# Feeding one stage of a fused attention and gMLP block: eight operand pieces reloaded in place, or twelve in two rings

## The chip, the core and the metric

The kernel runs on one NeuronCore of one Trainium2 chip. The metric is device time in microseconds, of one launch.

## What is computed

One transformer block with two parallel branches on 2048 tokens of width 512, in float32:

```python
xn = layernorm(x)                                   # x: 2048 x 512
q, k, v = split(xn @ wqkv)                          # 32 heads of 16
A = softmax(q @ k.T * 16**-0.5) @ v, heads joined, @ wo
z = gelu(xn @ w_in)                                 # 2048 x 1792
z1, z2 = z[:, :896], layernorm(z[:, 896:])
B = (z1 * (w_sp @ z2 + b_sp)) @ w_out               # w_sp: 2048 x 2048
out = x + A + B
```

## The kernel before

Dense products are made in three float32r passes (high times high, low times high, high times low), each operand held as a high and a low part. The contraction of 128 rows is cut into an upper and a lower half of 64 rows, which run side by side in PE as two matmuls into two PSUM banks, `dps0` and `dps1`. One such pair of matmuls is a *slot* (`dense_slot`, L1456).

Two streams of work share PE. Attention goes through 16 pairs of heads, each with four groups of 512 queries and 16 steps: maxima (M, L1405), scores (S, L1391), exponentials on ACT, and value products (V, L1499). The dense stream is a queue of generators: the values' projection, q and k (`qk_rest`), z2 (`z2_all`, 16 token tiles), z1 (`z1_all`), the product with w_sp (`spatial`), w_out (`mlp_out`) and wo (`attn_out`). The strings `ORDER` say by hand in which order S, M, V and dense slots (D) follow each other; one string is a row, and each row ends in a V.

The whole program is laid out ahead of time by a planner in Python. It keeps an estimated clock for each engine (`T`), and writes an instruction when its planned time has come; loads are asked for by small generators, which wait for room in a pool of buffers (`piece`, `room`), for a *road* that spaces large loads (`clear`, `bulk`), or for a planned time (`later`). The chip then keeps to the written order on each engine, and only semaphores decide when an instruction starts. All loads and nearly all stores go through SP's one queue (`move`, L169), in the order written. In the built program each transfer of that queue waits for the landing of the one eight places before it, so eight are under way at most.

The stage around the change is z1: z1 transposed, 896 rows in seven blocks of 128 (f), by four groups g of 512 tokens. `W1 = ((0, 1), (2, 3), (4, 5), (6, 6))` pairs the blocks: unit u works on two blocks, one in the upper half of PE's rows and one in the lower. Units 0 to 2 take both blocks from the same g; unit 3, the odd block 6, takes group g-1 in the upper half and g in the lower, once for each odd g. So the order of units is 0 1 2 (g = 0), 3 0 1 2 (g = 1), 0 1 2 (g = 2), 3 0 1 2 (g = 3): 14 units of eight steps j. A step needs the piece `xp` j of the normalised, transposed x: 64 upper rows for one block and 64 lower rows for the other, each a load of 256 KB from DRAM (`xscr`), and a half of the unit's weights `w1p` (two loads of 256 KB from `w1scr`).

There are eight buffers `xp0` to `xp7`. `fetch_first` (L628) fills them once, beginning with the last of z2's tiles. Afterwards `x_next` (L615) reloads an upper or a lower half in place, right after the step that used it last: the lower halves after unit 2 of an even g, the upper halves after unit 3, both after unit 2 of an odd g. `xat[j]` is the planned time at which piece j is in (`LOADX` = 6.0 us after its issue). The eight `w1p` pieces are asked for by `fetch_w1` (L619) from three tiles before the end of z2 on, all of them ahead of x. At the same time other loads pass through SP's queue: at each change of the pair of heads eight parts of the next pair's *stacks* (`qst`, `kst`, `load_stacks` L926), once per group the row maxima of the scores, which DVE makes (`ms`), and which go out (`mscr<-ms`) and come back in two loads into the rows of q (`qst<-mscr`, `max_fin` L955), the stores of z2 and z1 (`z2scr`, `z1scr`), and eight kept pieces of w_sp (`fetch_parts`, `wf<-wsscr`, 512 KB each).

Of the kernel before, what the change touches and what calls it, by code (L numbers as in the profile page):

```python
# [22 lines left out]
NT = S // P  # L23
# [60 lines left out]
LOADX = 6.0  # L84
# [9 lines left out]
def fused_block(ctx, tc, x, wqkv, wo, w_in, w_spT, b_sp, w_out, out):  # L94
# [76 lines left out]
    def clock():  # L171
        return T["P"]
# [195 lines left out]
    def fetch_parts(out, k, scr, spare):  # L368
        yield "C", lambda: clear() and room["big"] + room["old"] > 1 + spare[0]
        bulk(2.0)  # L370
# [236 lines left out]
    xp, xat = {}, {}  # L607

    def x_half(g, j, rows):
        c, h = divmod(j, 2)  # L610
        for r in rows:
            move(xp[j][64 * r:64 * r + 64], xscr[g][c][64 * h:64 * h + 64])
        xat[j] = max(clock(), ends[0]) + LOADX

    def x_next(g, j, rows):  # L615
        xat[j] = FAR
        later(0.2, x_half, g, j, rows)

    def fetch_w1(u, i, spare):  # L619
        yield "C", lambda: clear() and room["big"] + room["old"] > 1 + spare[0]  # L620
        bulk(2.0)
        t = piece(f"w1p{u}_{i}", place(w1, (u, i)))
        for r, f in enumerate(W1[u]):
            move(t[64 * r:64 * r + 64].rearrange("p a (c h f) -> p a c h f", c=2, h=2), w1scr[:, f, :, 2 * i:2 * i + 2, :, :])
        yield "T", LOAD
        w1[u, i] = t

    def fetch_first():  # L628
        for j in range(2 * ND):
            yield "C", lambda: room["big"] + room["old"] > 2  # L630
            xp[j] = piece(f"xp{j}", place(xp, j))
            x_half(0, j, (0, 1))
        late1[0] = 1

    def z2_all():
        yield from need(lambda: len(w2) == 2 * ND)
        for t in range(NT):
# [6 lines left out]
            if t == NT - 3:  # L644
                for u in range(4):
                    for i in range(2):
                        spawn(fetch_w1(u, i, late1), 1)
            if t == NT - 1:
                spawn(fetch_first(), 1)
# [52 lines left out]
    def z1_all():  # L702
        for g in range(NG):
# [3 lines left out]
            for n, (u, lo, hi) in enumerate(pairs):  # L707
# [9 lines left out]
                yield from need(lambda: (u, 0) in w1 and (u, 1) in w1)  # L717
                for j in range(2 * ND):
                    yield from need(lambda: xat.get(j, FAR) <= clock(), 0.1)
                    c = slice(j % 4 * P, (j % 4 + 1) * P)  # L720
                    ops = lambda _: (w1[u, j // 4][:, 0, c], w1[u, j // 4][:, 1, c], xp[j][:, 0, :], xp[j][:, 1, :])
                    yield from dense(1, ops, ops, (0, 1), j == 0, j == 2 * ND - 1)
                    if u == 3:
                        x_next(g, j, (0,))
                    elif u == 2 and g == NG - 1:
                        later(0.7, leave, xp, j)
                    elif u == 2:
                        x_next(g + 1, j, (0, 1) if g % 2 else (1,))
# [899 lines left out]
```

## Time and profile before

| | |
|---|---|
| three runs | 1828.26, 1833.22, 1839.35 us (median 1833.22) |
| profiled execution | 1831.37 us, of which 1829.3 from the first to the last instruction |
| granted clock of PE over the span | 0.996 |
| busy: PE, DVE, ACT, POOL | 1790.8, 1443.7, 1212.6, 685.3 us |
| matmuls of z1 (`dps<-xp,w1p`) | 672, from 500.7 to 694.4 us |
| loads of x halves for z1 (`xp<-xscr`) | 64 of 256 KB, issued from 488.4 to 654.0 us |

A busy time is the union of an engine's instructions, so PE's 98% says that something runs on it, not that it runs at its peak. What one stage costs is read from that stage: from the distance between the same points of the schedule there and elsewhere, and from what ended each wait. In the rows of waits and of the timeline, the bracket at the end gives the idle time before the instruction and what ended it. "SPq" is SP's queue issuing a transfer; that row's duration is the issuing, not the transfer.

### The profile page before, as it was taken

What the parts mean: (1) busy time and instruction counts of PE and PEld (TensorE: products, weight loads), DVE (VectorE), ACT (ScalarE), POOL (GpSimd) and SP (SyncE); (2) the same over time, 40 slices, a digit from 0 to 9 for tenths busy, and PEclk for the clock granted to TensorE, in tenths of its full rate; (3) what the DMA queues carried; (4) which work ended last, traced back from release to release, by engine and by line L of the source; (5) the groups of instructions that cost most, each with busy time, mean ns of one, the idle gap of its engine ahead of it and who ended that gap; (6) DMA issues with size and microseconds to landing.
All of it is one profiled execution on the core that took longest, in us unless ns stands there. A gap on an engine that the chain in (4) does not pass through costs nothing.

```text
span 1829.3 us, 38128 instructions
## 1 busy us (share of the span) xinstructions
PE 1790.8 (98%) x14708; PEld 1083.9 (59%) x14708; DVE 1443.7 (79%) x1716; ACT 1212.6 (66%) x1329; POOL 685.3 (37%) x803
## 2 busy tenths in 40 slices
PE   9999999999999999999999999999999999999997
PEld 6665665665665556666565665656566565664542
DVE  8868788888887777888788777878778787887882
ACT  4357777888876767666666666666666666666655
POOL 5442142777787767222722270007020600011201
PEclk9999999999999999999999999999999999999999
DMA  7879854434987676775878497548856766583322
GB/s 265 285 229 310 260 182 111 131 109 121 241 200 223 159 190 176 195 174 164 225 188 197 140 223 169 140 121 223 183 143 175 206 158 146 135 199 96 105 87 81
DMA packets 257757, 323.18 MB, mean 177 GB/s; under 512 B 70096, under 2 KB 147472, under 8 KB 257568
## 3 DMA queue, kind: packets, MB, share of 16 engines
q1 hardware_dynamic: 250088, 293.49, 61.0%
q0 software_dynamic: 7488, 27.27, 4.6%
q8 instruction: 115, 1.88, 0.4%
q14 instruction: 66, 0.54, 0.1%
HBM read 206.36 MB, written 114.30 MB: 175 GB/s over the span
## 4 chain that ended last, share of the span: by engine, by line
PE 89%; DMA 4%; DVE 4%; ACT 1%; POOL 1%; issue 1%; SPq 0%; POOLq 0%; DVEq 0%; ACTq 0%
PE dps L1456 35%; PE sl L1499 24%; PE sl L1391 14%; PE sl L1405 12%; DVE mm L950 3%; DMA xp<-xscr 2%; DMA kst<-kscr 1%; ACT pf L111 1%; PE dps L1470 1%; PE sl L277 1%; PE sl L278 0%; PE sl L279 0%; DMA w1p<-w1scr 0%; PE sl L1456 0%; DVE bst L1175 0%
## 5 line engine op out<-in xcount | busy, mean ns | idle before, releaser
L950 DVE TENSOR_REDUCE mm<-sl 128x2 f32<-128x1024 f32 x1008 | 1207.2, 1222 | 182.3 <-PE sl L1405 172.4
L111 ACT ACTIVATE pf<-sl 128x1024 f32<-128x1024 f32 x1024 | 1042.9, 1026 | 347.2 <-PE sl L1391 309.8
L1391 PE MATMUL sl<-qst,kst 50*128 50x512 f32 x2048 | 433.8, 416 | 8.0 <-DVE mm L950 2.9
L1499 PE MATMUL sl<-pf,vhalf 128*32 128x512 f32 x3840 | 439.8, 597 | 0.9 <-DVE on L1085 0.7
L1405 PE MATMUL sl<-kst,qst 48*128 48x512 f32 x2016 | 416.0, 404 | 5.4 <-ACT pf L111 2.8
L1456 PE MATMUL dps<-wsp,zs 64*128 64x512 f32 x2352 | 382.6, 392 | 0.0
L1391 PEld LDWEIGHTS sl<-qst,kst 50*128 50x128 f32 x2048 | 195.0, 184 | 209.7 <-issue 75.2
L1405 PEld LDWEIGHTS sl<-kst,qst 48*128 48x128 f32 x2016 | 192.3, 185 | 115.7 <-ACT pf L111 53.0
L1499 PEld LDWEIGHTS sl<-pf,vhalf 128*32 128x32 f32 x3840 | 111.7, 110 | 251.4 <-issue 216.2
L1456 PEld LDWEIGHTS dps<-wsp,zs 64*128 64x128 f32 x2352 | 225.8, 187 | 35.6
L111 ACT ACTIVATE e<-sl 128x512 f32<-128x512 f32 x64 | 38.3, 599 | 185.5 <-PE sl L1499 162.0
L1529 DVE TENSOR_TENSOR e<-sl,e 128x512 f32<-128x512 f32 x64 | 44.3, 692 | 133.5 <-PE sl L1499 74.8
L848 POOL TENSOR_TENSOR hhl<-z1i,hhl 128x512 fp32r<-128x512 f32 x26 | 33.2, 1287 | 275.8 <-ACT hhl L111 254.8
L1456 PE MATMUL dps<-xp,w1p 64*128 64x512 f32 x672 | 113.2, 397 | 7.8 <-DMA xp<-xscr 7.8
L1456 PE MATMUL dps<-w,xt 64*128 64x448 f32 x768 | 113.0, 368 | 1.7
L1456 PE MATMUL dps<-wout,hp 64*128 64x512 f32 x672 | 110.1, 392 | 0.0
L1001 POOL TENSOR_TENSOR ob<-ob 128x512 f32<-128x512 f32 (+1 forms) x16 | 20.6, 1287 | 214.1 <-DMA ob<-rscr 195.4
L1456 PEld LDWEIGHTS dps<-w,xt 64*128 64x128 f32 x768 | 75.6, 186 | 15.3 <-issue 8.1
L1456 PEld LDWEIGHTS dps<-xp,w1p 64*128 64x128 f32 x672 | 66.6, 188 | 20.3 <-DMA xp<-xscr 11.0
L1456 PEld LDWEIGHTS dps<-wout,hp 64*128 64x128 f32 x672 | 64.8, 187 | 9.8
L467 POOL TENSOR_TENSOR qkhl<-qr,qkhl 128x512 fp32r<-128x512 f32 x24 | 30.4, 1284 | 85.4 <-ACT qkhl L111 40.5
L997 POOL TENSOR_TENSOR ob<-ob 128x512 f32<-128x512 f32 (+1 forms) x16 | 20.9, 1304 | 100.3 <-DMA ob<-escr 98.5
(252 smaller groups left out, 1618.4 us busy)
## 6 DMA issues: line engine op xcount, KB each, us to landing
zs<-z2scr SPq DMA_DIRECT2D x192, 256.0 KB
xp<-xscr SPq DMA_DIRECT2D x64, 256.0 KB
escr<-e SPq DMA_DIRECT2D x60, 256.0 KB
hscr<-hhl POOLq DMA_DIRECT2D x28, 512.0 KB, 6.8
qst<-qscr SPq DMA_DIRECT2D x60, 192.0 KB
kst<-kscr SPq DMA_DIRECT2D x60, 192.0 KB
qscr<-qkhl SPq DMA_DIRECT2D x16, 512.0 KB
kscr<-qkhl SPq DMA_DIRECT2D x16, 512.0 KB
```

The source lines that it names most:

```text
L111: return nc.scalar.activation(out, in_, func, **kw)
L277: nc.tensor.matmul(acc, lh, rh, start=first, stop=False)
L467: nc.gpsimd.tensor_sub(hl[:, 1, :], raw_, hl[:, 0, :].bitcast(F32))
L848: nc.gpsimd.tensor_sub(hl[:, 1, :], z1, hl[:, 0, :].bitcast(F32))
L950: nc.vector.tensor_reduce(mmax[g][:, :, t, kc], sl[k], AX.X, ALU.max)
L997: nc.gpsimd.tensor_add(both_[rows, 0, :], both_[rows, 0, :], both_[rows, 1, :])
L1001: nc.gpsimd.tensor_mul(both_[rows, 0, :], both_[rows, 0, :], both_[rows, 1, :])
L1391: nc.tensor.matmul(sl[k][:, j, :], kst[p % 2][rows, kt * P:(kt + 1) * P], qst[p % 2][rows, c * 512:(c + 1) * 512], start=True, stop=True)
L1405: nc.tensor.matmul(sl[k][:, j, :], qst[p % 2][rows, tt * P:(tt + 1) * P], kst[p % 2][rows, kc * 512:(kc + 1) * 512], start=True, stop=True)
L1456: nc.tensor.matmul(bank_of(bank)[:, :w], lhs, rhs, start=go, stop=stop)
L1499: nc.tensor.matmul(sl[k][cols:cols + VW, 0, :], vpack(p, kt + r, j), pf[:, j * 512:(j + 1) * 512], start=n % CYC == 0, stop=n % CYC == CYC ...
L1529: nc.vector.tensor_add(e, sl[k][:, 0, :], e)
```

## The change

Twelve buffers `xp0` to `xp11` take the place of eight. The upper halves form one ring over the twelve, the lower halves another: the half for group g and step j is number q = 8 g + j and goes to buffer q modulo 12, and it may be loaded when the half twelve before it has been used for the last time (`xgone`). One generator, `z1_loader`, asks for all 64 halves and the eight `w1p` pieces in the order in which the units need them (`x_due`). It begins four tiles of z2 before the end, not three (weights) or one (x). Each load waits for the planner's road, and takes 1.6 us of it (an x half) or 3.0 us (a weight piece), unless it is due within six steps of the present one. A step waits, in the plan, for the halves and the weights that it uses. `LOADX` goes from 6.0 to 7.0 us, and a kept piece of w_sp takes 3.0 us of the road and not 2.0. The arithmetic and the number of transfers stay.

```diff
-LOADX = 6.0
+LOADX = 7.0
+XRING = 12
+XBULK = 1.6
...
     def fetch_parts(out, k, scr, spare):
         yield "C", lambda: clear() and room["big"] + room["old"] > 1 + spare[0]
-        bulk(2.0)
+        bulk(3.0 if out is wsp else 2.0)
...
-    xp, xat = {}, {}
...
-    def x_next(g, j, rows):
-        xat[j] = FAR
-        later(0.2, x_half, g, j, rows)
-
-    def fetch_w1(u, i, spare):
...
-    def fetch_first():
-        for j in range(2 * ND):
-            yield "C", lambda: room["big"] + room["old"] > 2
-            xp[j] = piece(f"xp{j}", place(xp, j))
-            x_half(0, j, (0, 1))
-        late1[0] = 1
+    xp, xat, slot = {}, {}, []
+    at_x, xgone = [-FAR], [0, 0]
+
+    def x_uses():
+        n = 0
+        for g in range(NG):
+            for u in ((3, 0, 1, 2) if g % 2 else (0, 1, 2)):
+                yield n, u, g - 1 if u == 3 else g, g
+                n += 1
+
+    def x_due():
+        seen, due = set(), []
+        for n, u, *gs in x_uses():
+            for j in range(2 * ND):
+                for r in (0, 1):
+                    if (r, gs[r], j) not in seen:
+                        seen.add((r, gs[r], j))
+                        due.append((8 * n + j, 1, r, 8 * gs[r] + j))
+            for i in range(2):
+                if ("w", u, i) not in seen:
+                    seen.add(("w", u, i))
+                    due.append((8 * n + 4 * i, 0, u, i))
+        return sorted(due)
+
+    def z1_loader():
+        for d, is_x, p, q in x_due():
+            soon = lambda: clear() or d <= at_x[0] + 6
+            if is_x:
+                k, (g, j) = q % XRING, divmod(q, 2 * ND)
+                c, h = divmod(j, 2)
+                yield "C", lambda: soon() and q < xgone[p] + XRING and (k in xp or room["big"] + room["old"] > 1 + late1[0])
+                bulk(XBULK)
+                if k not in xp:
+                    xp[k] = piece(f"xp{k}", place(xp, k))
+                move(xp[k][64 * p:64 * p + 64], xscr[g][c][64 * h:64 * h + 64])
+                xat[p, q] = max(clock(), ends[0]) + LOADX
+            else:
+                yield "C", lambda: soon() and room["big"] + room["old"] > 1 + late1[0]
+                bulk(3.0)
...
+                w1[p, q] = t
...
-            if t == NT - 3:
-                for u in range(4):
-                    for i in range(2):
-                        spawn(fetch_w1(u, i, late1), 1)
+            if t == NT - 4:
+                spawn(z1_loader(), 1)
             if t == NT - 1:
-                spawn(fetch_first(), 1)
+                late1[0] = 1
...
-                yield from need(lambda: (u, 0) in w1 and (u, 1) in w1)
                 for j in range(2 * ND):
-                    yield from need(lambda: xat.get(j, FAR) <= clock(), 0.1)
+                    at_x[0] = 8 * unit + j
+                    pu, pl = 8 * lo + j, 8 * hi + j
+                    yield from need(lambda: all(xat.get(k, FAR) <= clock() for k in ((0, pu), (1, pl), ("w", u, j // 4))), 0.1)
...
+                    xu, xl, wt = xp[pu % XRING], xp[pl % XRING], w1[u, j // 4]
...
-                    if u == 3:
-                        x_next(g, j, (0,))
-                    elif u == 2 and g == NG - 1:
-                        later(0.7, leave, xp, j)
-                    elif u == 2:
-                        x_next(g + 1, j, (0, 1) if g % 2 else (1,))
+                    if u == 3 or u == 2 and lo % 2:
+                        later(0.2, xgone.__setitem__, 0, pu + 1)
+                    if u == 2:
+                        later(0.2, xgone.__setitem__, 1, pl + 1)
```

In the built program DVE's and ACT's instructions stand in the same order as before, and so do PE's matmuls, but for the names of some buffers. What moves is SP's queue. In the rows below `xp`, `w1p`, `xt`, `wf`, `qst` and `kst` are loads, `z2scr`, `z1scr`, `escr` and `mscr` stores, and the first number of a name is that of the buffer or part.

First place: SP's queue at the end of z2, where tile 15's operand (`xt15`) is loaded and the stacks of the next pair follow. Before, from the last row of `xt15` on:

```order
L169 DMA xt15_5346<-xscr3_3_127 128x2x128
L169 DMA z2scr_129<-z2hl9_1_5279 128x3x128
L169 DMA w1p0_0_5355<-w1scr_186 64x2x512 x2
L169 DMA qst0_100<-qscr1_105 48x1024
L169 DMA kst0_102<-kscr1_109 48x1024
L169 DMA w1p0_1_5387<-w1scr_186 64x2x512 x2
L169 DMA qst0_100<-qscr1_105 48x1024
L169 DMA qst1_101<-mscr2_176 2x16x32 x2
L169 DMA w1p1_0_5418<-w1scr_186 64x2x512 x2
L169 DMA kst0_102<-kscr1_109 48x1024
L169 DMA qst0_100<-qscr1_105 48x1024
L169 DMA kst0_102<-kscr1_109 48x1024
```

Now, the rows ahead of `xt15`, and then those behind it:

```order
L171 DMA w1p0_0_5180<-w1scr_186 64x2x512 x2
L171 DMA escr0_0_142<-e3_0_5010 128x512
L171 DMA xp0_5231<-xscr0_0_112 64x1024 x2
L171 DMA xp1_5275<-xscr0_0_112 64x1024 x2
L171 DMA z2scr_129<-z2hl9_0_5205 128x4x128
L171 DMA xp2_5325<-xscr0_1_113 64x1024 x2
L171 DMA z2scr_129<-z2hl9_0_5205 128x4x128
L171 DMA mscr2_176<-ms14_5322 128x32
L171 DMA z2scr_129<-z2hl9_1_5287 128x3x128
L171 DMA xt15_5358<-xscr3_0_124 128x2x128
```

```order
L171 DMA xt15_5358<-xscr3_3_127 128x2x128
L171 DMA z2scr_129<-z2hl9_1_5287 128x3x128
L171 DMA qst0_100<-qscr1_105 48x1024
L171 DMA kst0_102<-kscr1_109 48x1024
L171 DMA qst0_100<-qscr1_105 48x1024
L171 DMA qst1_101<-mscr2_176 2x16x32 x2
L171 DMA kst0_102<-kscr1_109 48x1024
L171 DMA qst0_100<-qscr1_105 48x1024
L171 DMA kst0_102<-kscr1_109 48x1024
L171 DMA z2scr_129<-z2hl10_0_5347 128x4x128
L171 DMA qst0_100<-qscr1_105 48x1024
L171 DMA xp3_5485<-xscr0_1_113 64x1024
```

Half of unit 0's weights and the first three x pieces, both halves, went ahead of `xt15`; no weights of z1 stand among the stacks any more, and the fourth x piece does.

Second place: SP's queue at the change of pair after the first three units of z1, up to the store of the maxima. Before:

```order
L169 DMA xp3_5796<-xscr1_1_117 64x1024
L169 DMA qst1_101<-qscr1_105 48x1024
L169 DMA xp4_5799<-xscr1_2_118 64x1024
L169 DMA xp5_5817<-xscr1_2_118 64x1024
L169 DMA kst1_103<-kscr1_109 48x1024
L169 DMA xp6_5820<-xscr1_3_119 64x1024
L169 DMA qst1_101<-qscr1_105 48x1024
L169 DMA xp7_5829<-xscr1_3_119 64x1024
L169 DMA kst1_103<-kscr1_109 48x1024
L169 DMA qst1_101<-qscr1_105 48x1024
L169 DMA mscr1_175<-ms17_6350 128x32
L169 DMA kst1_103<-kscr1_109 48x1024
```

Now:

```order
L171 DMA qst1_101<-qscr1_105 48x1024
L171 DMA xp2_5325<-xscr1_3_119 64x1024
L171 DMA kst1_103<-kscr1_109 48x1024
L171 DMA xp3_5485<-xscr1_3_119 64x1024
L171 DMA qst1_101<-qscr1_105 48x1024
L171 DMA xp8_6114<-xscr1_0_116 64x1024
L171 DMA xp9_6137<-xscr1_0_116 64x1024
L171 DMA xp10_6159<-xscr1_1_117 64x1024
L171 DMA kst1_103<-kscr1_109 48x1024
L171 DMA qst1_101<-qscr1_105 48x1024
L171 DMA mscr1_175<-ms17_6356 128x32
L171 DMA kst1_103<-kscr1_109 48x1024
```

Before, the lower halves of group 1 (`xscr1`) for `xp0` to `xp7` stand among the stacks, all eight between the end of z2's stores and `mscr`; now four of them do (`xp0` to `xp3`, as numbers 12 to 15), the four others were loaded ahead of the stretch into `xp8` to `xp11`, and three upper halves come before `mscr`, where none came. From the first of these x halves to `mscr` there are 18 transfers before and 16 now; right ahead of them now stands the last weight piece, `w1p3_1`, in two transfers.

Third place: SP's queue at the change of pair in the last group. Before:

```order
L169 DMA qst0_100<-qscr1_105 48x1024
L169 DMA xp4_5799<-xscr3_2_126 64x1024
L169 DMA xp5_5817<-xscr3_2_126 64x1024
L169 DMA kst0_102<-kscr1_109 48x1024
L169 DMA xp6_5820<-xscr3_3_127 64x1024
L169 DMA qst0_100<-qscr1_105 48x1024
L169 DMA wf5_5_7577<-wsscr5_183 128x1024
L169 DMA xp7_5829<-xscr3_3_127 64x1024
L169 DMA kst0_102<-kscr1_109 48x1024
L169 DMA qst0_100<-qscr1_105 48x1024
L169 DMA mscr1_175<-ms21_7604 128x32
```

Now:

```order
L171 DMA xp5_5762<-xscr3_2_126 64x1024
L171 DMA kst0_102<-kscr1_109 48x1024
L171 DMA xp6_5810<-xscr3_3_127 64x1024
L171 DMA qst0_100<-qscr1_105 48x1024
L171 DMA xp7_5847<-xscr3_3_127 64x1024
L171 DMA kst0_102<-kscr1_109 48x1024
L171 DMA wf1_1_7566<-wsscr1_179 128x1024
L171 DMA qst0_100<-qscr1_105 48x1024
L171 DMA wf1_1_7594<-wsscr2_180 128x1024
L171 DMA kst0_102<-kscr1_109 48x1024
L171 DMA qst0_100<-qscr1_105 48x1024
L171 DMA mscr1_175<-ms21_7602 128x32
```

Before, the upper halves of group 3 (`xscr3`) go through the whole stretch, the last one behind a piece of w_sp; now their last one stands ahead of two such pieces, and the first four stand before the stretch. From the first transfer of the stretch (`xp0` before, `z1scr2` now) to `mscr` there are 18 transfers before and 15 now.

More of the change, by code (lines that the diff above doesn't have):

```diff
@@ L606, in fused_block @@
     W1 = ((0, 1), (2, 3), (4, 5), (6, 6))
-    xp, xat = {}, {}
[L609 to L613, printed above, removed]
-    def x_next(g, j, rows):
-        xat[j] = FAR
-        later(0.2, x_half, g, j, rows)
-    def fetch_w1(u, i, spare):
[L620 to L626, printed above, removed]
@@ new lines, in z1_loader @@
+    def z1_loader():
[13 more added lines that the diff above has]
+                bulk(3.0)
+                t = piece(f"w1p{p}_{q}", place(w1, (p, q)))
+                for r, f in enumerate(W1[p]):
+                    move(t[64 * r:64 * r + 64].rearrange("p a (c h f) -> p a c h f", c=2, h=2), w1scr[:, f, :, 2 * q:2 * q + 2, :, :])
+                xat["w", p, q] = max(clock(), ends[0]) + LOAD
+                w1[p, q] = t
@@ L702, in z1_all @@
     def z1_all():
+        unit = 0
         for g in range(NG):
@@ L716, in z1_all @@
                     calm[0] = True
-                yield from need(lambda: (u, 0) in w1 and (u, 1) in w1)
                 for j in range(2 * ND):
-                    yield from need(lambda: xat.get(j, FAR) <= clock(), 0.1)
+                    at_x[0] = 8 * unit + j
+                    pu, pl = 8 * lo + j, 8 * hi + j
+                    yield from need(lambda: all(xat.get(k, FAR) <= clock() for k in ((0, pu), (1, pl), ("w", u, j // 4))), 0.1)
                     c = slice(j % 4 * P, (j % 4 + 1) * P)
-                    ops = lambda _: (w1[u, j // 4][:, 0, c], w1[u, j // 4][:, 1, c], xp[j][:, 0, :], xp[j][:, 1, :])
-                    yield from dense(1, ops, ops, (0, 1), j == 0, j == 2 * ND - 1)
-                    if u == 3:
-                        x_next(g, j, (0,))
-                    elif u == 2 and g == NG - 1:
-                        later(0.7, leave, xp, j)
-                    elif u == 2:
-                        x_next(g + 1, j, (0, 1) if g % 2 else (1,))
+                    xu, xl, wt = xp[pu % XRING], xp[pl % XRING], w1[u, j // 4]
+                    au, al = (wt[:, 0, c], wt[:, 1, c], xu[:, 0, :], xu[:, 1, :]), (wt[:, 0, c], wt[:, 1, c], xl[:, 0, :], xl[:, 1, :])
+                    yield from dense(1, lambda _: au, lambda _: al, (0, 1), j == 0, j == 2 * ND - 1)
+                    if u == 3 or u == 2 and lo % 2:
+                        later(0.2, xgone.__setitem__, 0, pu + 1)
+                    if u == 2:
+                        later(0.2, xgone.__setitem__, 1, pl + 1)
+                    if g == NG - 1 and (u == 2 or u == 3 and pu + XRING >= 2 * ND * NG):
+                        later(0.7, leave, xp, pu % XRING)
                 if g == NG - 1:
@@ L731, in z1_all @@
                         leave(w1, (u, i))
+                unit += 1
                 yield "e", [z1_out(f, h, i) for i, (f, h) in enumerate(zip(W1[u], (lo, hi)))]
```

## The prediction

> **What bounds the kernel now.** I read the page's busy shares and the chain that ended last first, then who PE waited for, then those waits in PE's timeline, and last SP's queue around them.
>
> ```profile
> PE 1790.8 (98%) x14708; PEld 1083.9 (59%) x14708; DVE 1443.7 (79%) x1716; ACT 1212.6 (66%) x1329; POOL 685.3 (37%) x803
> PE 89%; DMA 4%; DVE 4%; ACT 1%; POOL 1%; issue 1%; SPq 0%; POOLq 0%; DVEq 0%; ACTq 0%
> ...
> PE dps L1456 <- DMA xp<-xscr: 7.8, 5, 3.9
> PE sl L1391 <- DMA qst<-mscr: 0.7, 1, 0.7
> ```
>
> PE is the bound: busy for 98% of the span and 89% of the chain. An edit that leaves PE's instructions as they are can therefore only win what PE waits, and the waits on this change's transfers are 7.8 us in five pieces (the last two rows are from the table of who waited for whom: total, times, longest). PE's timeline shows where they stand, in brackets, with a sixth on a row of maxima:
>
> ```profile
> 472.05 0.69 PE L1391 MATMUL sl<-qst,kst 50*128 50x512 f32 x2 [0.67 <-DMA qst<-mscr]
> ...
> 508.24 0.73 PE L1456 MATMUL dps<-xp,w1p 64*128 64x512 f32 x3 [0.52 <-DMA xp<-xscr]
> 510.32 0.50 PE L1456 MATMUL dps<-xp,w1p 64*128 64x512 f32 x2 [0.54 <-DMA xp<-xscr]
> ...
> 551.95 0.50 PE L1456 MATMUL dps<-xp,w1p 64*128 64x512 f32 x2 [1.17 <-DMA xp<-xscr]
> ...
> 567.28 0.50 PE L1456 MATMUL dps<-xp,w1p 64*128 64x512 f32 x2 [1.65 <-DMA xp<-xscr]
> ...
> 664.84 1.22 PE L1456 MATMUL dps<-xp,w1p 64*128 64x512 f32 x4 [3.91 <-DMA xp<-xscr]
> ```
>
> Idle time is not the whole loss, because PE runs slower after a long wait and small waits of the weight loads do not show as PE idle. The whole loss is read from the pitch of the schedule: every row of the hand-written order ends in one block of value matmuls (L1499), so the starts of these blocks are a ruler.
>
> ```profile
> 440.39 3.64 PE L1499 MATMUL sl<-pf,vhalf 128*32 128x512 f32 x32
> ...
> 467.75 2.78 PE L1499 MATMUL sl<-pf,vhalf 128*32 128x512 f32 x24
> ...
> 496.58 3.64 PE L1499 MATMUL sl<-pf,vhalf 128*32 128x512 f32 x32
> 511.68 1.90 PE L1499 MATMUL sl<-pf,vhalf 128*32 128x512 f32 x13
> ...
> 538.45 1.92 PE L1499 MATMUL sl<-pf,vhalf 128*32 128x512 f32 x16
> ...
> 569.14 2.35 PE L1499 MATMUL sl<-pf,vhalf 128*32 128x512 f32 x20 [0.18 <-ACT pf L111]
> ...
> 648.99 1.49 PE L1499 MATMUL sl<-pf,vhalf 128*32 128x512 f32 x12
> ...
> 681.98 2.35 PE L1499 MATMUL sl<-pf,vhalf 128*32 128x512 f32 x20
> ...
> 908.78 1.49 PE L1499 MATMUL sl<-pf,vhalf 128*32 128x512 f32 x12
> ...
> 935.42 1.92 PE L1499 MATMUL sl<-pf,vhalf 128*32 128x512 f32 x16
> ...
> 660.00:680.00 20.00, 16.09 (x118) 8.95 (x118) 10.74 (x10) 10.44 (x13) 9.50 (x10) 0.83 0.86 218
> ```
>
> Two rows take 27.36 us in the z2 stage (440.39 to 467.75) and 26.64 where nothing waits later (908.78 to 935.42). Against that: (a) 467.75 to 496.58 takes 28.83, 1.47 too much, the tail of z2; (b) 496.58 to 511.68, one row, takes 15.10 against 13.68, 1.42 too much, the first unit of z1; (c) 538.45 to 569.14 takes 30.69, 4.05 too much; (d) 648.99 to 681.98 takes 32.99, 6.35 too much. Of (d) 3.91 is the wait; the other 2.44 is PE's clock, which the last row (a window of 20 us: PE, PEld, DVE, ACT, POOL, clock, DMA share, GB/s) gives as 0.83 of full. No wait of 1.65 or less did that. Sum of the losses: 1.47 + 1.42 + 4.05 + 6.35 = 13.29 us.
>
> **Why the transfers are late.** The chain names the issue and the time to landing of the transfers on which PE waited, and SP's queue shows what it held:
>
> ```profile
> 502.46 7.81 DMA xp<-xscr
> ...
> 540.57 11.34 DMA xp<-xscr
> ...
> 560.97 6.27 DMA xp<-xscr
> ...
> 654.03 10.76 DMA xp<-xscr
> ...
> SPq L169 <- DMA xp<-xscr: 21.0, 32, 1.5
> ...
> 440.00:460.00 20.00, 19.48 (x166) 11.60 (x168) 16.91 (x27) 17.08 (x22) 13.68 (x24) 1.00 0.40 113
> 460.00:480.00 20.00, 18.87 (x162) 13.21 (x160) 16.79 (x21) 16.05 (x18) 15.08 (x20) 1.00 1.01 204
> 540.00:560.00 20.00, 18.84 (x156) 11.18 (x150) 13.31 (x15) 13.07 (x16) 18.64 (x25) 1.00 1.01 200
> ...
> 529.93 0.51 SPq L169 DMA_DIRECT2D xp<-xscr  x1
> ...
> 544.86 0.34 SPq L169 DMA_DIRECT2D mscr<-ms  x1
> ...
> 553.82 1.35 SPq L169 DMA_DIRECT2D qst<-mscr  x2
> ...
> 640.60 0.44 SPq L169 DMA_DIRECT2D xp<-xscr  x1
> ...
> 657.56 0.34 SPq L169 DMA_DIRECT2D mscr<-ms  x1
> ...
> 666.28 1.34 SPq L169 DMA_DIRECT2D qst<-mscr  x2
> ```
>
> Issue plus landing gives 510.27, 551.91, 567.24 and 664.79: to within 0.1 us where the waits end. From 529.93 to 540.57 SP issued 16 transfers, and the last landed at 551.91: 1.37 us each, DMA share 1.01 in that window. From 640.60 to 654.03 it issued 16 again, landing at 664.79: 1.51 us each. So z1's pieces stand in a full line, together with the next pair's stacks (qst, kst), and a piece that moves out of that stretch brings all behind it forward by about 1.4 us. SP itself waited 21.0 us in 32 pieces for older xp transfers (window 440 to 700), the sign that its line of eight outstanding transfers was full.
>
> **The change part by part.** PE, DVE and ACT keep their instructions in the same order: DVE's and ACT's are equal row by row, PE's differ only in the names of wsp pieces; POOL moves one store's issue by a place. No engine's work changes: 0 us. The number of transfers stays too (64 x halves, 16 for w1). What moves is SP's line.
>
> - *Twelve pieces instead of eight.* The first four pieces of each next group of 512 columns find room before the old group is used up. Of the eight lower halves that stood between 529.93 and 540.57, four now stand ahead of that stretch: 4 x 1.37 = 5.5 us earlier for the last lower half, against a wait of 1.17, and as much for the upper halves behind it, against 1.65. (c) goes: -4.05. Before the last boundary it is the same with 4 x 1.51 = 6.0 against 3.91: (d) goes, with its clock: -6.35. If a half freed only half of that, 0.7 us, 2.8 would clear (c) and leave 1.1 of (d) without the clock loss; I take the measured spacing.
> - *Order of need, four tiles ahead.* The first half of unit 0's weights and three pieces of x move in front of tile 15's operand, and the weights of units 1 and 2, which stood ahead of all of x, move behind it: eight transfers of w1 out of the way of a last piece that was 0.54 late. (b) goes: -1.42. The eight transfers moved forward need 8 x 1.37 = 11.0 us of a stretch whose DMA share was 0.40 (440 to 460), so that 12 of its 20 us were free: no cost, by 1 us. If that cover were gone, the stacks of the next pair, which begin at the end of that stretch, would be late by the overhang. They also get rid of the w1 transfers between them (four ahead of the max rows that PE waited 0.67 for), so (a) goes, -1.47; its other end is 0.
> - *Fetching kept wsp pieces less often* (3.0 for 2.0 of road time): seven of the eight now stand later, most of them behind the last x pieces, and the last right behind the store of 673.94. The first use is at 699.31, so 0 us; some zs and wsp loads of spatial change places too, and PE's table has no wait on either. LOADX and XBULK are numbers of the planner; since PE's order did not change, 0.
>
> ```profile
> 673.94 0.45 SPq L169 DMA_DIRECT2D z1scr<-z  x1
> ...
> 699.31 0.40 PE L1456 MATMUL dps<-wf,zs 64*128 64x512 f32 x2
> ```
>
> - *What is late next.* At a pair's boundary PE's score matmuls need the row maxima, which go through DRAM: mscr<-ms, then two qst<-mscr, in the same line of SP, and SP stands still at the second until the first has landed (544.86 to 553.82, and 657.56 to 666.28). Before, PE's own waits for x hid this.
>
> ```profile
> 556.94 0.50 PE sl L1391 x2
> ```
>
> This is the chain's first score after the value block: PE found the maxima there by 556.94, 3.1 us after the issue at 553.82. About half of (c), 2.0 us, lies before that, so PE will come at 554.9. In the new line 16 transfers stand between the start of the stretch and mscr<-ms, not 18: 2.7 us less; but one w1 piece, two transfers, now stands right in front of the stretch: 2.7 us more. With these cancelling, PE waits 2.0. Lower end 0 (w1's transfers are done before). Upper end: if these rows take the 6.27 of a queued transfer instead of about 3, 2.0 + 3.3 = 5.3, plus the 2.44 of the clock, 7.7. At the second boundary PE would come at 671.9 - 6.35 = 665.6 and the maxima, 3.1 after 666.28, at 669.4: 3.8 late, but 15 transfers stand ahead instead of 18, 3 x 1.51 = 4.5 earlier. Margin 0.7: I put 0.5 for it. Together +2.5, nearest to what the rows of the same place give.
>
> Sum: -13.29 + 2.5 = -10.8. The profiled execution took 1831.37 us (span 1829.3), so 1820.6, given as 1821. It is 1.85 below the median of the three runs, 1833.22, which spread from 1828.26 to 1839.35; measured against that median the gain would read a little larger.
>
> A rule to weigh here: the Trainium skill ("TensorE: Matmul & The Clock Gate", Part 1) has the clock halve after an idle window of about 3.4 us. The trace only brackets it, between 1.65 and 3.91. By that rule the new wait of 2.0 costs nothing more; if the edge stood below 2.0, it would cost up to 2.44 more and the sum were 1823. No run here has shown which yet. Another: "DMA: Bandwidth & Descriptors" (Anatomy of one DMA) prices a transfer at about 2.0 us fixed plus bytes over 436 GB/s, an estimate of 0.6 us for a 256 KB half. By it four halves bring 2.4, 1.5 of (d) stays, and the sum is 1822; the trace has 1.37 to 1.51, and I go by it.
>
> **The rivals.**
> 1. *The maxima become the wait.* At the first boundary 7.7 instead of 2.0, by the same line that made xp late: gain 13.29 - 7.7 - 0.5 = 5.1, 1826. For it: SP's standing still for 9 us at both places. Against: fewer transfers ahead of them.
> 2. *Slower.* The same chain at both boundaries and at each x handover in between, because the paced loader leaves the line full for longer: it decides from 13.3 us of new waits on. Two waits of 7.7 are 15.4: 1833.5; with (a) not won either and the clock lost once more, 1837.4. Against: DVE's and PE's orders stay, and the one wait on maxima in PE's table is the 0.67 of 472.05.
> 3. *It doesn't do what it says.* If the line's rate is the limit wherever the pieces stand, the halves that went ahead are paid for by the w1 pieces that come later, and (a), (b) and (c) only change places. Then only (d), with its wsp transfer of 512 KB in front of the last x half, is won: 6.35, 1825. For it: a DMA share of 1.01 in two of the windows above. Against: 0.40 in the window that the loads move into.
>
> **How the numbers follow.** Forecast 0.61 (own range 1815 to 1825); rival 1 0.16; rival 2 0.08; rival 3 0.15. Less than 0.5%, 9.2 us, can hardly be told from no change here. Faster is below 1824.0: nine tenths of the forecast, 0.54, and little else, with the spread of runs taking as much from it as it adds. Slower is above 1842.4: rival 2 with a bad spread, 0.05. Same: 0.41. The range holds the forecast and the rivals 1 and 3 and is widened below by the 3 us that runs lay under the profiled one, and above to the edge of rival 2: 1814 to 1832.
>
> **What would show it.** Right: no bracket <-DMA xp on L1456 over 0.3 us; two rows near 26.6 from 511 on; clock 1.00 in every window; one bracket <-DMA qst<-mscr near 555 of about 2 us. Wrong: that bracket over 3.5 with a clock below 1.00 (rival 1), such brackets at two places (2), or xp brackets that have only moved (3).

## The result, and the profile after

The changed kernel took 1821.51 us (median of six runs, 1818.38 to 1823.02) against 1830.11 us (six runs, 1828.26 to 1839.35) for the kernel before on the same chip: a ratio of 0.9942 with a 95% interval of 0.9922 to 0.9962 (the ratios on record here and below differ by up to 0.1%, some 2 us, from the quotient of the two medians). The forecast was 1821. Its profiled execution took 1822.65 us and has a span of 1820.8 us, 8.5 less than the one before.

From the page after, the row of busy times and the chain by engines; then the one row on z1's transfers that is left in the table of who PE waited for; and that wait in PE's timeline:

```profile
PE 1788.2 (98%) x14708; PEld 1084.1 (60%) x14708; DVE 1443.1 (79%) x1716; ACT 1212.6 (67%) x1329; POOL 685.1 (38%) x803
PE 91%; DVE 4%; DMA 3%; ACT 1%; issue 1%; POOL 0%; POOLq 0%; SPq 0%; DVEq 0%; ACTq 0%
...
PE sl L1412 <- DMA qst<-mscr: 2.0, 1, 2.0
...
555.83 0.59 PE L1412 MATMUL sl<-qst,kst 50*128 50x512 f32 x2 [1.99 <-DMA qst<-mscr]
```

PE waits for x nowhere any more; in the place of the five brackets of before there is one, on the row maxima. The places (a) to (d) are those of the prediction, stretches of the ruler: (a) the end of z2, (b) the first unit of z1, and (c) and (d) the two changes of the pair of heads inside z1, called the boundaries below. The ruler of the prediction, the starts of the value blocks (now L1520), shows what that was worth place by place:

```profile
469.63 3.64 PE L1520 MATMUL sl<-pf,vhalf 128*32 128x512 f32 x32
...
497.03 3.21 PE L1520 MATMUL sl<-pf,vhalf 128*32 128x512 f32 x28
...
510.65 3.64 PE L1520 MATMUL sl<-pf,vhalf 128*32 128x512 f32 x32
...
537.25 3.64 PE L1520 MATMUL sl<-pf,vhalf 128*32 128x512 f32 x32
...
567.53 2.78 PE L1520 MATMUL sl<-pf,vhalf 128*32 128x512 f32 x24
...
647.46 2.78 PE L1520 MATMUL sl<-pf,vhalf 128*32 128x512 f32 x24
...
674.12 3.64 PE L1520 MATMUL sl<-pf,vhalf 128*32 128x512 f32 x32
```

(a) took 27.40 instead of 28.83, 1.43 less; (b) 13.62 instead of 15.10, 1.48 less; (d) 26.66 instead of 32.99, 6.33 less. (c) still takes 30.28 instead of 30.69: it lost its x waits and got the new one. In the windows the clock of the first boundary is below full, the one of the second is full (before it was 0.83 there):

```profile
540.00:560.00 20.00, 18.01 (x146) 12.29 (x136) 12.52 (x12) 12.24 (x14) 19.06 (x26) 0.93 1.04 227
...
660.00:680.00 20.00, 20.00 (x172) 11.05 (x170) 15.64 (x19) 14.22 (x19) 14.81 (x16) 1.00 0.76 229
```

The chain, in order of time, names what the new wait hangs on: start, time to landing, transfer.

```profile
533.54 8.28 DMA kst<-kscr
...
541.88 8.84 DMA mscr<-ms
...
550.78 4.91 DMA qst<-mscr
```

mscr<-ms moves 16 KB, and takes 8.84 us to land, behind a half stack (kst) that took 8.28.

The four places sum up to 1.43 + 1.48 + 0.41 + 6.33 = 9.65 us; the span fell by 8.5. Of these 9.65, 1.78 were lost at the run's start, which the change does not touch, and some 0.6 were won in small pieces elsewhere, 0.3 of it in the second row after (d). At the start PE waited for a stack of the first pair in this execution and not in the one of before, and the value block that began at 85.29 began at 87.07.

```profile
57.36 0.46 PE L1290 MATMUL dps<-kst,qst 48*128 48x512 f32 x1 [0.53 <-DMA kst<-kscr]
...
85.29 3.64 PE L1499 MATMUL sl<-pf,vall 128*32 128x512 f32 x32
...
87.07 3.21 PE L1520 MATMUL sl<-pf,vall 128*32 128x512 f32 x28
```

In the executions below, which all have the same instructions up to there, that block starts between 85.05 and 86.99. So some 1.8 us of the difference between the two profiles is the run's own, and places are compared, not ends.

### The profile page after: what moved, and what is told of

Its sections match the earlier page's. It is cut to its first block, busy times and chain, and to the rows that moved or that the text cites. A ratio compares the mean times of both kernels' runs of the same rounds, so it can differ in the third digit from the quotient of the medians.

```text
span 1820.8 us, 38108 instructions
## 1 busy us (share of the span) xinstructions
PE 1788.2 (98%) x14708; PEld 1084.1 (60%) x14708; DVE 1443.1 (79%) x1716; ACT 1212.6 (67%) x1329; POOL 685.1 (38%) x803
## 4 chain that ended last, share of the span: by engine, by line
PE 91%; DVE 4%; DMA 3%; ACT 1%; issue 1%; POOL 0%; POOLq 0%; SPq 0%; DVEq 0%; ACTq 0%
PE dps L1477 36%; PE sl L1520 25%; PE sl L1412 14%; PE sl L1426 13%; DVE mm L971 3%; ACT pf L113 1%; DMA kst<-kscr 1%; PE dps L1491 1%; DMA mscr<-ms 0%; DVE bst L1196 0%; PE sl L1477 0%; DMA qscr<-qkhl 0%; PE sl L279 0%; DMA qst<-mscr 0%; PE sl L1116 0%
## 5 line engine op out<-in xcount | busy, mean ns | idle before, releaser
L1520 PE MATMUL sl<-pf,vhalf 128*32 128x512 f32 x3840 | 438.7, 595 | 0.8 <-DVE on L1106 0.7
L1520 PEld LDWEIGHTS sl<-pf,vhalf 128*32 128x32 f32 x3840 | 111.5, 109 | 249.6 <-issue 214.2
```

The costliest lines, as they stand in the source:

```text
L1520: nc.tensor.matmul(sl[k][cols:cols + VW, 0, :], vpack(p, kt + r, j), pf[:, j * 512:(j + 1) * 512], start=n % CYC == 0, stop=n % CYC == CYC ...
```

## The experiments

The theory from the prediction: PE's order is fixed, and what is lost is lateness of transfers in one full line of DMA; the change wins by taking transfers out of two stretches. The rival inside it: the halves come late because no buffer is free for them (room), not because the line is full (crowding). And the new wait on maxima could be SP's queue, the DMA engines, or the stacks that stand there.

In every kernel with x and w1 PE's, DVE's and ACT's orders are those of the two kernels compared. To keep them so, where the loader is altered, the planner's own landing times for x and w1 are set to zero; this alone changes no queue's order:

```diff
-LOADX = 7.0
+LOADX = 0.0
...
-                xat["w", p, q] = max(clock(), ends[0]) + LOAD
+                xat["w", p, q] = max(clock(), ends[0])
```

| kernel | us, median (range) | before beside it | ratio, 95% interval |
|---|---|---|---|
| the change | 1821.51 (1818.38 to 1823.02) | 1830.11 | 0.9942, 0.9922 to 0.9962 |
| eight buffers | 1837.53 (1834.63 to 1843.64) | 1831.94 | 1.003, 1.0017 to 1.0042 |
| weights first | 1826.25 (1824.89 to 1828.7) | 1831.94 | 0.996, 0.9945 to 0.9975 |
| begun two tiles ahead | 1820.68 (1819.47 to 1822.84) | 1831.94 | 0.9929, 0.9913 to 0.9946 |
| maxima by POOL | 1831.21 (1829.16 to 1834.06) | 1831.94 | 0.9991, 0.998 to 1.0002 |
| stacks behind the boundary | 1819.22 (1817.42 to 1820.69) | 1832.33 | 0.9926, 0.9914 to 0.9939 |
| the kernel before with them there | 1826.01 (1824.73 to 1826.38) | 1832.33 | 0.9965, 0.9953 to 0.9976 |
| eight buffers and stacks behind | 1823.1 (1818.3 to 1826.0) | 1832.33 | 0.9949, 0.9935 to 0.9962 |
| before with late weights | 1836.92 (1833.58 to 1843.64) | 1831.63 | 1.0028, 1.0016 to 1.004 |
| the change again | 1822.62 (1821.08 to 1825.12) | 1831.63 | 0.9951, 0.9939 to 0.9964 |
| stacks behind, begun two ahead | 1818.46 (1817.72 to 1820.72) | 1831.63 | 0.993, 0.9918 to 0.9942 |

### Parts of the change undone

Eight buffers:

```diff
-XRING = 12
+XRING = 8
```

> The changed kernel with eight buffers for x instead of twelve; loader, order of need and start stay, and PE's, DVE's and ACT's orders are those of the changed kernel. Theory A (room: the first pieces of the next group of columns must have buffers that are not those in use): the waits at the two boundaries return on L1477 near 551 and 660, up to the (c) 4.05 and (d) 6.35 of the kernel before, and hide the maxima's 3.66 again: some 6.7 us slower than the changed kernel's 1821.5, about 1828, and at least 1825 if the paced order takes half of it. Theory B (the order of need and the early start are what helps, the room is idle): within 1.5 us of 1821.5. In both, (a) and (b) stay won: rows of 13.6 from 470 to 511.

1837.53 us, slower than the kernel before, and 16 us above the changed one by either measure (0.9% in the ratios). Who PE waited for, and three of the seven waits in its timeline:

```profile
PE dps L1477 <- DMA xp<-xscr: 11.7, 7, 5.2
...
554.84 1.22 PE L1477 MATMUL dps<-xp,w1p 64*128 64x512 f32 x3 [5.22 <-DMA xp<-xscr]
...
614.32 0.50 PE L1477 MATMUL dps<-xp,w1p 64*128 64x512 f32 x2 [1.37 <-DMA xp<-xscr]
...
670.48 0.73 PE L1477 MATMUL dps<-xp,w1p 64*128 64x512 f32 x4 [3.57 <-DMA xp<-xscr]
```

The direction is that of theory A, the size more than twice what it said (16 for 6.7), and it came with a third place, near 614. So the paced loader needs the four more pieces: with eight it waits more than the old loader did with the same eight (11.7 us for 7.8).

Weights first (the key of the list of needs):

```diff
-                    due.append((8 * n + 4 * i, 0, u, i))
+                    due.append((0, 0, u, i))
```

> The changed kernel with all weights of z1 due ahead of all x pieces, as they stood before; twelve buffers and the start four tiles ahead stay. Theory A (my step on order: twelve w1 transfers in front of x make its last pieces late): (b) returns, +1.4 us, brackets <-DMA xp near 500 to 511, 1823. Theory B (the early start alone has paid for (b): 16 us more for the same transfers): no bracket, 1821.5 within 0.7. (a) is a finer sign: by theory A max rows near 472 stand behind w1 transfers again and a bracket <-DMA qst<-mscr of about 0.7 comes back.

```profile
PE dps L1477 <- DMA xp<-xscr: 2.8, 6, 0.7
...
495.03 3.64 PE L1520 MATMUL sl<-pf,vhalf 128*32 128x512 f32 x32
...
504.26 0.50 PE L1477 MATMUL dps<-xp,w1p 64*128 64x512 f32 x1 [0.66 <-DMA xp<-xscr]
...
515.12 1.06 PE L1520 MATMUL sl<-pf,vhalf 128*32 128x512 f32 x8
```

1826.25, by the ratios 3.3 us above the changed kernel, though the two intervals overlap: theory A, and more than its 1.4. The ruler says more than the total. The row of (b), from 495.03 to 515.12, takes 20.09 us where the changed kernel takes 13.62, 6.5 more; x brackets are back in it (the sum of the six is 2.8), with a record of half clock of 3.41 us at 506.3. In return the wait on maxima is gone, and (c) takes 26.66 us instead of 30.28. The bracket on the max rows near 472 did not return, so that finer sign failed: ten of the sixteen weight transfers were issued by 452, and no other before 477. The first x half was issued at 490.8 only (at 447.6 in the changed kernel), so this edit takes the early start from x as well as its place in the order, and does not part the two.

Begun two tiles ahead:

```diff
-            if t == NT - 4:
+            if t == NT - 2:
                 spawn(z1_loader(), 1)
```

> The changed kernel with the loader begun two tiles of z2 ahead instead of four (about 27 us later); order of need and twelve buffers stay. Theory A (the start pays (b) and the room in the 440 to 460 window is what makes it free): 12 of the 18 first transfers come into the stretch whose DMA share was above 0.8, x brackets of 0.5 to 1.5 us in the first unit return, +1.4, 1823. Theory B (order of need is enough, since a unit uses its pieces over 13.7 us): 1821.5 within 0.7. Theory C (late transfers push the next pair's stacks and maxima back): the wait on maxima grows from 2.0 to over 4 and the sum is above 1824.

```profile
562.32 0.50 PE L1477 MATMUL dps<-xp,w1p 64*128 64x512 f32 x2 [1.16 <-DMA xp<-xscr]
```

0.9929 against 0.9942, each interval holding the other's value: theory B. The first unit has no x bracket; the wait on maxima is gone, and one of 1.16 on x stands at 562. So the two tiles more buy nothing that can be measured: the order of need, begun two tiles ahead, is enough for (b), and (a) went here as well.

### What the wait on maxima hangs on

The maxima by POOL's queue while z1 runs (move is SP's dma_start; carry is used for mscr<-ms and the two qst<-mscr):

```diff
+    in_z1 = [False]
+
+    def carry(dst, src):
+        (nc.gpsimd if in_z1[0] else nc.sync).dma_start(raw(dst), raw(src))
```

> The changed kernel with the row maxima's way through DRAM (mscr<-ms and two qst<-mscr) issued by POOL's queue instead of SP's while z1 runs (seven groups, 21 transfers); all else stays. Theory A (the new wait is SP's line: mscr<-ms took 8.84 us to land and was issued 2.6 after ms was ready): the bracket <-DMA qst<-mscr of 1.99 and its 1.67 of clock go, 3.66 less, 1817.9. Theory B (the DMA engines are full whichever queue asks, share 1.04): the maxima land no earlier, 1821.5 within 1. Theory C (POOL standing still for the landing makes the gelu products late, and DVE's or ACT's work behind them): new waits on PE, 1823 or more.

```profile
PE sl L1418 <- DMA qst<-mscr: 7.1, 6, 3.2
...
541.72 0.70 POOL L176 DMA_DIRECT2D mscr<-ms  x1
...
550.53 1.32 POOL L176 DMA_DIRECT2D qst<-mscr  x2 [4.08 <-DMA mscr<-ms]
...
DMA to landing us min/median/max: 2.7/2.9/8.5
```

Theory A fell. From POOL's queue the 16 KB land 8.5 us after their issue at 541.72; from SP's queue they took 8.84. The last row is for the seven such stores from POOL's queue: five of them, away from the boundaries, took 2.7 to 3.0 us, and the two at the boundaries 8.5 and 7.9. So it is not their place in SP's queue that makes them late but what is in flight there, whichever queue asks: theory B for the mechanism. The DMA engines are the likely place, with a share of 1.04 there in the changed kernel; no run tells them apart from the memory behind them. The price is another: POOL came to the issue no earlier than SP (541.72 against 541.88) and stood still for 4.08, and PE had six waits on maxima, 7.1 us in all; the ratios make it 9 us slower than the changed kernel.

Then whatever fills the engines there must go. While z1 runs (in_z1 is set and cleared at the ends of z1_all), the next pair's stacks, asked for at the first chance (529.9), are held to score step 28, behind the boundary:

```diff
-            if p + 1 < NP and stacks[0] <= p and i >= (3 if p else 20) and (i >= LATE or calm[0] and not owed[0]):
+            if p + 1 < NP and stacks[0] <= p and i >= (3 if p else 20) and (i >= 28 if in_z1[0] else (i >= LATE or calm[0] and not owed[0])):
```

> The changed kernel with one condition altered: while z1 runs, the next pair's stacks (eight qst and kst transfers, issued from 529.9 to 543.1 in the changed kernel, first needed by PE near 590) are asked for at score step 28 of a pair, behind the boundary, instead of at the first chance. Theory A (the maxima are late because the stacks stand with the x halves in a full line; POOL's queue gave the same 8.8 us, so the line is the DMA engines' own): 8 x 1.37 = 11 us less ahead of mscr<-ms and qst<-mscr, the bracket of 1.99 and its clock go, 3.66 less than the changed kernel, a ratio to before of about 0.992. Theory B (the x halves alone fill it): the wait stays above 1, ratio 0.994. Theory C (the stacks are what is late next): new brackets <-DMA kst or qst<-qscr near 590 or 700 of 1 to 4 us, ratio 0.995 to 0.998.

SP's queue (issues) and the ruler of PE there:

```profile
539.17 0.33 SPq L171 DMA_DIRECT2D mscr<-ms  x1
545.46 1.34 SPq L171 DMA_DIRECT2D qst<-mscr  x2
...
537.13 3.64 PE L1522 MATMUL sl<-pf,vhalf 128*32 128x512 f32 x32
...
550.10 3.64 PE L1522 MATMUL sl<-pf,vhalf 128*32 128x512 f32 x32
563.75 3.64 PE L1522 MATMUL sl<-pf,vhalf 128*32 128x512 f32 x32
```

Theory A: mscr<-ms lands within 6.3 us, qst<-mscr is issued 5.3 us earlier, and (c) takes 26.62 instead of 30.28. That is the whole 3.66 us, with no wait on x, maxima or stacks left in z1. The ratio, 0.9926, is that of theory A, though its interval overlaps the changed kernel's; the row is the firmer evidence.

### Crowding or room

The same condition in the kernel before, with its eight buffers and its own loaders:

> The kernel before with that same condition alone: eight buffers, its own loaders and its own order, only the next pair's stacks moved behind the boundary. Theory A (crowding: the losses at the boundaries come from the line, and any 11 us taken out of it clears them): (c) 4.05 and (d) 6.35 go, (a) and (b) stay, some 10 us less, ratio 0.9945, without a twelfth buffer. Theory B (room: a half can only be asked for once its buffer is free, and that is too late by itself): brackets <-DMA xp of 0.5 or more stay at both boundaries, less than half of 10.4 is won, ratio above 0.997.

```profile
PE dps L1459 <- DMA xp<-xscr: 2.8, 5, 0.6
...
537.72 3.64 PE L1502 MATMUL sl<-pf,vhalf 128*32 128x512 f32 x32
...
564.29 3.64 PE L1502 MATMUL sl<-pf,vhalf 128*32 128x512 f32 x32
...
588.68 11.30 SPq L169 DMA_DIRECT2D xp<-xscr  x12
...
590.91 3.64 PE L1502 MATMUL sl<-pf,vhalf 128*32 128x512 f32 x32
...
608.44 3.64 PE L1502 MATMUL sl<-pf,vhalf 128*32 128x512 f32 x32
```

(c) takes 26.57, 4.1 less, (d) takes 26.61 instead of 32.99, and no x bracket is left at either boundary, with eight buffers. So at the boundaries it is crowding, not room. But the time fell by 0.35% only: the stacks now stand at 575 to 582, ahead of the burst of twelve x halves of 588.68, which come late by four brackets of 0.53 to 0.62 near 600, and the row from 590.91 takes 17.53, where it took 12.97 before. 4.56 us were given back at a new place. Brackets are half of that; the rest shows in no wait of PE. The total lies between the two theories.

> The changed kernel with eight buffers (which lost some 16 us against twelve) and with the stacks behind the boundary. Theory A (crowding): the x brackets, 11.7 us in all with eight buffers, fall under 2 us together, ratio 0.993. Theory B (room): the 5.2 near 552 stays above 2.5 and the ratio is 0.997 or more.

```profile
PE dps L1479 <- DMA xp<-xscr: 2.2, 4, 0.6
```

The diff is that of the eight buffers and that of the stacks together. The 5.22 near 555 has gone, theory A; four brackets of 0.37 to 0.61 near 600 stay, with a record of half clock, and the ratio of 0.9949 lies between the two forecasts. Against the same kernel with twelve pieces (0.9926) this is the price of the smaller ring once the boundaries are free: some 4 us, near the place where the stacks now stand. There the twelve pieces still count.

The weights of units 1 to 3 behind the first x pieces in the kernel before:

```diff
-                for u in range(4):
-                    for i in range(2):
-                        spawn(fetch_w1(u, i, late1), 1)
+                for i in range(2):
+                    spawn(fetch_w1(0, i, late1), 1)
             if t == NT - 1:
                 spawn(fetch_first(), 1)
+                for u in range(1, 4):
+                    for i in range(2):
+                        spawn(fetch_w1(u, i, late1), 1)
```

> The kernel before with the weights of units 1 to 3 asked for behind the first x pieces (six pieces, twelve transfers); eight buffers, places of the stacks and all else as before. Theory A (my steps on (a) and (b): w1 stands in front of the max rows near 472 and of the last x pieces near 508): both go, 2.9 less, ratio 0.9984; the brackets 0.67 at 472 and 0.52 and 0.54 at 508 to 511 vanish. Theory B (the x pieces begin too late, at 488, whatever stands ahead): (b) stays, only (a) may go, ratio 0.999 to 1.0. (c) and (d) stay by both.

```profile
474.80 0.76 PE L1393 MATMUL sl<-qst,kst 50*128 50x512 f32 x2 [1.47 <-DMA qst<-mscr]
506.85 0.95 PE L1393 MATMUL sl<-qst,kst 50*128 50x512 f32 x2 [4.28 <-DMA qst<-mscr]
...
486.37 0.34 SPq L169 DMA_DIRECT2D mscr<-ms  x1
...
490.35 7.58 SPq L169 DMA_DIRECT2D xp<-xscr  x10
498.64 1.77 SPq L169 DMA_DIRECT2D qst<-mscr  x2
```

Both theories missed: 0.28% slower. The x halves did come closer together, twelve of them between the two steps of the maxima, and PE waited 4.28 us for maxima instead of 1.06 for x. (a) did not go: its bracket grew from 0.67 to 1.47. This kernel keeps unit 0's weights, four transfers, between the two steps of those max rows, as before, which may be why; no run here moves these alone. So in this form, without the pacing, the order of need only changed what was late.

### The clock

> No part of the reference: PE runs 57 bursts of 44 to 59 equal matmuls (128x512) and waits between two of them for a chain on DVE, made for waits of about 1.0 to 3.4 us, each four times at other times of day; x is copied to the output. Theory A (the clock is judged in fixed windows of 3.41 us, as the two records of half clock so far, 3.41 and 6.83 long, suggest: PE idle for about half of one window halves the next): no wait under 1.4 drops it, every wait of 3.4 does, and between them it depends on how the wait lies across a window's edge, so that the same length gives both answers. Theory B (length decides, with an edge between 1.65 and 1.99): all waits above 1.99 drop it and none under 1.65, whatever their place. Theory C (an idle window of 3.4 us is needed): only waits near 3.4 and above drop it. A drop costs PE at most 3.41 / 2 = 1.7 us.

This kernel and the next leave out the whole block; a "drop" is a record of half clock in the trace. Most long operations on DVE had run ahead, and of the waits only five were over 0.5 us: 1.45 (no drop), 2.05, 2.66, 3.21 and 4.91 (a drop each). The chain was then tied to the end of each burst:

> The kernel of bursts and waits again, with the DVE chain tied to the end of each burst, since in the first form most long operations ran ahead and only five waits of over 0.5 us came about (1.45 us: no drop; 2.05, 2.66, 3.21 and 4.91: a drop each). 56 waits of about 0.8 to 3.5 us, each length four times. Theory A (fixed windows of 3.41 us, the idle share inside one window decides): a wait of 1.8 to 2.4 drops the clock where it lies in one window and not where an edge splits it in halves; below 1.4 never, above 3.4 always. Theory B (length alone, edge between 1.45 and 1.99): the four waits of each length agree. Theory C (3.4 us of idle time needed) has already failed at 2.05 here and at 1.99 in the changed kernel.

Seventeen of the 56 waits were followed by half clock, in records of 3.41 us (once two in a row), all on one grid. Four waits and the clock in the window after each (windows: length, PE, PEld, DVE, POOL, clock, DMA share, GB/s):

```profile
308.78 13.47 PE L80 MATMUL acc<-rhs,wt 128*128 128x512 f32 x51 [1.82 <-DVE rhs L85]
...
511.71 12.99 PE L80 MATMUL acc<-rhs,wt 128*128 128x512 f32 x56 [1.82 <-DVE rhs L85]
...
199.06 11.18 PE L80 MATMUL acc<-rhs,wt 128*128 128x512 f32 x48 [3.12 <-DVE rhs L85]
...
603.21 15.05 PE L80 MATMUL acc<-rhs,wt 128*128 128x512 f32 x58 [3.12 <-DVE rhs L85]
...
310.24:313.65 3.41, 3.41 (x9) 2.63 (x8) 0.00 (x0) 0.00 (x0) 0.50 0.00 0
511.63:515.04 3.41, 3.33 (x15) 2.75 (x16) 0.03 (x1) 0.00 (x0) 1.00 0.00 0
...
201.01:204.42 3.41, 3.41 (x17) 2.81 (x15) 0.00 (x0) 0.00 (x0) 1.00 0.02 5
603.78:607.19 3.41, 3.41 (x10) 2.64 (x9) 0.00 (x0) 0.00 (x0) 0.50 0.00 0
```

A wait of 1.82 halves the clock and another of 1.82 does not; a wait of 3.12 does not, where the grid's edge splits it into 1.65 and 1.47, and does, where 2.84 of it lie in one window. Theory A, for this kernel: PE idle for about half of one window of 3.41 us halves the next. With the grid laid 0.24 us ahead of the records (fitted), all 56 agree on whether a drop begins: the largest idle time in a window without a drop is 1.72 us, the smallest with one 1.77. It does not tell when the clock returns: the second of the two records in a row, at 624.3, follows a window with only 1.0 to 1.3 us idle.

The whole kernel does not keep to that edge. On the grid of the records PE was idle for 1.07 us (eight buffers with the stacks behind, 603.29 to 606.71), 1.30 (maxima by POOL, from 638.51) and 1.44 (late weights, from 556.31) in the window just ahead of a drop, and for 1.44 (late weights, from 672.36) and 1.39 (the changed kernel again, from 552.37) in windows that no drop followed. So PE's idle time, as the trace models it, does not decide alone there.

### The change again, and a version that beats it

> The changed kernel itself, to stand beside the next kernel on one chip. Ratio to before 0.994; the wait on maxima near 555 between 1.5 and 2.5 us and, if half clock follows it by the window that it falls in, one record of 3.41 us in some executions and none in others.

```profile
555.03 0.70 PE L1412 MATMUL sl<-qst,kst 50*128 50x512 f32 x2 [1.39 <-DMA qst<-mscr]
```

The same wait was 1.39 here, a little shorter than expected, and no half clock followed: that part of the new wait's price is there in one execution and not in the other. (c) took 28.30 us, 1.7 above the 26.62 of the kernel with the stacks moved.

> The changed kernel with the stacks behind the boundary (which alone gave 0.9926) and the loader begun two tiles ahead instead of four (which alone gave 0.9929 and a bracket of 1.16 on x at 562). Theory A (both only take crowding out of the same stretch): no better than the stacks alone, 0.992 to 0.993, no wait on x or maxima in z1; then four tiles are worth nothing once the stacks have gone. Theory B (the later start moves x into the stretch and the bracket on x near 562 comes back): 0.9935 or more.

1818.46, with no wait on x, maxima or stacks in z1, by the ratio (0.993) no different from the stacks alone (0.9926): theory A. Beside the changed kernel on the same chip it is 4.2 us faster (1817.72 to 1820.72 against 1821.08 to 1825.12).

## Why the prediction was right, step by step

- *What bounds, and the ruler.* Right. The losses put down to (a), (b), (c) and (d), 13.29 us, were all there to be won: 1.43 + 1.48 + 6.33 in the changed kernel, and 30.69 - 26.62 = 4.07 for (c) in the kernel with the stacks moved, 13.31 together.
- *The new wait.* Right in place and size, 1.99 for 2.0, but by two errors that cancel, which is luck. PE came at 553.84, not 554.9, and the maxima at 555.69, not 556.9; that alone is no error, since the whole schedule stood 1.2 us earlier there (537.25 for 538.45). Counted from that point, the last step of the maxima was issued 1.8 us earlier than before (13.53 for 15.37 us behind it), as if the w1 piece in front of the stretch, priced at 2.7 us, cost nothing; and the rows took 4.91 us to come instead of the 3.1 assumed, 1.8 more. "In the same line of SP" was the wrong line: from POOL's queue the store took 8.5 us where SP's took 8.84.
- *Its clock.* This is the step that failed: the sum takes the new wait at 2.0 and its clock at nothing ("By that rule the new wait of 2.0 costs nothing more"). (c) holds 3.66 us of new loss, of which the wait is 1.99 and 1.67 the clock, and the sign "clock 1.00 in every window" failed with 0.93. The edge of about 3.4 us of idle time that the Trainium skill gives ("TensorE: Matmul & The Clock Gate", Part 1) is too high here; about half of a window was enough. The trace of before held a sign of it: of the wait of 3.91, 1.7 us lay in the window (659.25 to 662.66) after which the half clock began, and the prediction read the edge as a length between 1.65 and 3.91, not as a share of a window.
- *The second boundary.* 0.5 put in, 0 found. New loss 3.66 instead of 2.5; the sum is -9.65 at these four places instead of -10.8. The start of the profiled run, 1.8 later by chance, and the 0.6 won elsewhere made -8.5 of it. So the profiled execution, to which the sum belongs, came out at 1822.65, two more than the 1820.6 of the sum; that the median, 1821.51, lies so close to 1821 is in part luck, since the six runs spread over 4.6 us.
- *Twelve pieces.* Right for this loader: with eight it loses 16 us. But "a piece that moves out of that stretch brings all behind it forward" holds for the stacks as well: with them out of it, eight buffers clear (c) and (d) in the kernel before. At the boundaries the ring is one way out of the crowd, not the cure of a lack of room; near 600 the smaller ring still costs some 4 us. By the price that the Trainium skill gives ("DMA: Bandwidth & Descriptors", Anatomy of one DMA, where it is a fit for transfers that GpSimd issues) 1.5 us of (d), an estimate, would have stayed. None did: (d) took 26.66 us, as the measured spacing said.
- *Order of need, four tiles ahead.* (b) went, and with the weights first, which also starts x late, it comes back. Four tiles instead of two cost nothing, as forecast, and brought nothing that can be measured. (a) went in every kernel with the new loader, whatever the order in it or its start. In all of them no w1 piece stands between the two steps of those max rows any more, which are 6.4 us apart in the changed kernel's queue (below) and were 9.7 apart before (455.51 and 465.20, four w1 transfers between them).

```profile
457.36 0.34 SPq L171 DMA_DIRECT2D mscr<-ms  x1
...
463.74 1.36 SPq L171 DMA_DIRECT2D qst<-mscr  x2
```

- *The rivals.* Rival 1 had the right place and too high a price, 3.66 for 7.7; the mechanism can come near it, as the waits of 3.20 by POOL's queue and 4.28 with the late weights show. Rival 2 would have needed that at several places, rival 3 that (a), (b) and (c) stay. Neither came, but at (c) alone rival 3 was nearly right: with the new loss only 0.41 was won there.

## What to carry to other kernels

Where transfers of several kinds share the DMA engines, ask of a late one not which buffer or queue it lacks but what else is in flight in the 10 us before it, and whether any of that is wanted later: here eight transfers needed near 590 were asked for at 530. A small transfer that the bound engine needs soon, such as row maxima through DRAM, is the first to suffer, and changing its queue did not help here. A gain read as a pitch of the schedule, place by place, tells what a median of runs hides: here 1.8 us of start and 1.7 us of clock came and went from run to run.

## What the runs showed of the hardware

- In the kernel of bursts the PE clock went by fixed windows of 3.41 us: 1.77 us or more without work in one window halved the next and 1.72 or less did not, at a cost of up to 1.7 us. In the whole kernel the wait of 1.99, all in one window, cost 3.66 in one execution, and that of 1.39 cost 1.7 in another, without a drop; but there windows with only 1.07 to 1.44 us idle were followed by half clock too.
- In six of the twelve profiled executions of the whole kernel a record of half clock stands between 1716 and 1751, where PE has no wait over 0.5 us; each costs up to 1.7 us, half of its 3.41. Why it comes there is open. So is the record in the kernel with the weights first, where the waits in one window come to about 1.1 us, and the others after small waits named above.
- 16 KB took 8.5 to 8.8 us to land from either of two queues while x halves and stacks were in flight, and 2.7 to 3.0 from POOL's queue at the five places where no stacks were.
